# Eight experts as nested conditional blocks of 2x2 products, seven for eight

## The chip, the cores and the metric

The kernel runs on one core of a Trainium2 chip. A core has engines with instruction streams of their own: TensorE for matrix products (PE in the profile, and PEld for the loading of its weights, the operand that stays in the array), VectorE (DVE), ScalarE (ACT), GpSimd (POOL) and SyncE (SP), which here issues transfers. Work moves between memory (DRAM), an on-chip store of 128 partitions (SBUF), and the banks into which TensorE accumulates (PSUM). The metric is the time of one execution on the device in microseconds, the median of several.

## The reference

A sliding-window attention feeds a mixture of experts with one expert per token. Cut to what matters:

```python
q, k, v: (8, 8, 576, 64)                      # batch, heads, positions, head size
scores = q @ k.T / 8, masked to 0 <= i - j < 64
x = softmax(scores) @ v                       # as (4608, 512): one row per token
logits = x @ w_gate                           # (4608, 8)
expert = argmax(logits); gate = softmax(logits)[expert]
for e in range(8):                            # w1[e]: (512, 1024), w2[e]: (1024, 512)
    y[expert == e] = relu(x[expert == e] @ w1[e]) @ w2[e]
out = gate[:, None] * y                       # all in float32
```

With these inputs the experts get 669, 400, 748, 505, 592, 390, 566 and 738 tokens. In chunks of 128 tokens that is 6, 4, 6, 4, 5, 4, 5 and 6, 40 in all. The kernels learn these counts only while they run.

## The kernel before

The program has four stages. The attention computes x for two batches at a time and writes it to DRAM (x_dram); on the way TensorE also forms the logits. The routing, on DVE with some matmuls, ranks the tokens within their experts. Each expert's share starts at a new tile of 128 tokens, so a token's slot is the start of its expert plus its rank; products of one-hot matrices (lo and hi, L467 to L471) give for each slot the token's number (perm_i) and its gate (gate_s). Slots without a token hold a number behind the last token, which the scatter leaves out.

The third stage goes over tiles of 128 slots. For tile i, `fetch` (L497) lets SP read the tile's expert and a flag, and load that expert's w1 and w2 (2 MB each) into one of three buffers where the flag says that the buffer holds another expert (L501, L502); POOL gathers the 128 rows of x by perm_i (L503). `turn` (L508) transposes the rows on TensorE (four transposes, L511), and DVE copies them to SBUF (L512). `work` (L514) computes the hidden layer with its features on the partitions, in two halves of 512 features (32 matmuls of 128 tokens in all; each float32 matmul is two instructions in the profile), applies the relu on DVE for one half (L530) and on ACT for the other (L528), lets TensorE turn the next tile, computes the output (8 matmuls of 512 columns, L535), lets ACT multiply by the gate (L539) and POOL scatter the rows to the output (L541).

There can be up to 43 tiles. The first 36 are written out without a condition; the rest stand in conditional blocks of two tiles (L556), which compare the number of tiles in use with a constant. With 40 tiles in use, the blocks for 36 and 38 run and the ones for 40 and 42 are jumped over.

The order on SP in this stage is as written (manual_schedule); the other engines' order is chosen by the framework's scheduler from what is written and when buffers come free. Tiles name buffers, and the framework puts in the waits between engines.

The fourth stage is the end: the last scatters land, and all engines meet.

## Time and profile before

| what | value |
| --- | --- |
| median of 3 runs (lowest, highest) | 904.05 us (903.75, 904.51) |
| the profiled execution's own time | 907.11 us |
| its span in the profile | 905.4 us |
| granted clock of TensorE, mean | 0.957 |
| attention | 0 to about 262 us |
| routing | about 262 to 312 us |
| tiles of the experts | 312 to 892 us, 580 us |
| end | 892 to 905.4 us |
| TensorE busy over the span | 843.1 us, 93% |
| hidden layer, L523 | 2560 instructions, 294.4 us |
| output, L535 | 640 instructions, 281.3 us |

How to read the profile: the busy time of an engine is the time in which its instructions ran; in a group of instructions the number behind x is the count, then come busy time, the mean of one in ns, and the idle time just before them with what ended it. Matmuls overlap in the pipeline of TensorE, so the mean of one (276 ns for L523) is longer than the distance from one to the next (112 ns in the timeline). The granted clock is 1.00 at full speed; 0.50 is half of it. The span begins with the first instruction and ends with the last; the time of the execution is a little longer.

### The profile page before, as it was taken

The numbers are of one execution on the slowest core, as the hardware profiler recorded it, in microseconds if no ns is written. First come the engines' busy times: TensorE is split into PE (matmuls) and PEld (weight loads), VectorE is DVE, ScalarE is ACT, GpSimd is POOL, SyncE is SP. The second block draws the span as 40 slices with busy tenths as digits, with TensorE's granted clock in tenths as the row PEclk, the third lists the DMA queues.
The fourth block names the chain that finished last, engine by engine and source line by source line (L and its number), as shares of the span: only waits on it lengthen the run. The fifth ranks groups of instructions, "written<-read, shape, count | busy, mean of one in ns | idle before, by whom it ended". The sixth has DMA issues, their size and how long they took to land. (4 is left out here: it accounts for less than half of the span.)

```text
span 905.4 us, 16347 instructions
## 1 busy us (share of the span) xinstructions
PE 843.1 (93%) x6668; PEld 617.7 (68%) x6668; DVE 231.6 (26%) x500; ACT 181.7 (20%) x486; POOL 124.6 (14%) x177
## 2 busy tenths in 40 slices
PE   7997999998953699999999999999999999999993
PEld 5775776776733577686767777686777768677772
DVE  4664665664655000000101000010101001010100
ACT  4553554553510000001000000010000001000000
POOL 3111111011000201111111111111111111101010
PEclk9998999998985599999999999999999999999998
DMA  6668677886020661793951494891794871880110
GB/s 139 150 163 200 142 190 193 212 221 160 3 105 0 235 230 36 280 320 144 315 212 47 148 347 165 308 315 39 240 321 156 314 256 36 316 294 23 36 47 11
DMA packets 164863, 159.99 MB, mean 177 GB/s; under 512 B 118320, under 2 KB 118320, under 8 KB 164786
## 3 DMA queue, kind: packets, MB, share of 16 engines
q1 hardware_dynamic: 153362, 129.01, 45.8%
q0 software_dynamic: 6560, 20.45, 6.2%
q10 hardware_dynamic: 4864, 9.44, 3.1%
q8 instruction: 55, 0.90, 0.4%
q14 instruction: 22, 0.18, 0.1%
HBM read 219.69 MB, written 19.92 MB: 265 GB/s over the span
## 5 line engine op out<-in xcount | busy, mean ns | idle before, releaser
L523 PEld LDWEIGHTS hp<-xgT,w 128*128 128x128 f32 x2560 | 294.1, 193 | 18.8 <-issue 18.7
L523 PE MATMUL hp<-xgT,w 128*128 128x128 f32 x2560 | 294.4, 276 | 0.0
L535 PE MATMUL yp<-w,hT 128*128 128x512 f32 x640 | 281.3, 592 | 0.0
L535 PEld LDWEIGHTS yp<-w,hT 128*128 128x128 f32 x640 | 118.5, 190 | 133.9 <-issue 133.9
L530 DVE TENSOR_SCALAR hT<-hp 128x512 f32<-128x512 f32 x40 | 27.7, 692 | 390.9 <-PE hp L523 390.9
L237 ACT ACTIVATE pr<-sc,mx 128x128 f32<-128x128 f32 x288 | 79.4, 375 | 71.9 <-DVE mx L234 53.3
L528 ACT ACTIVATE hT<-hp 128x512 f32<-128x512 f32 x40 | 23.9, 597 | 310.2 <-PE hp L523 310.2
L541 POOL DMA_INDIRECT out_dram<-y,perm_i x40 | 40.6, 1016 | 316.7 <-ACT y L539 303.2
L539 ACT ACTIVATE y<-yp,gate_s 128x512 f32<-128x512 f32 x40 | 27.5, 687 | 266.1 <-PE yp L535 266.1
L503 POOL DMA_INDIRECT xg<-x_dram,perm_i x42 | 41.0, 975 | 235.6 <-PE tp L511 179.2
L512 DVE COPY xgT<-tp 128x512 f32<-128x512 f32 x41 | 28.3, 691 | 137.2 <-PE tp L511 137.2
L234 DVE TENSOR_REDUCE mx<-sc 128x3 f32<-128x384 f32 x96 | 49.1, 553 | 42.5 <-PE sc L227 41.1
L246 PE MATMUL tr<-ident,pr 128*128 128x128 f32 x288 | 49.5, 287 | 0.1
L246 PEld LDWEIGHTS tr<-ident,pr 128*128 128x128 f32 x288 | 34.7, 146 | 20.1 <-ACT qT L190 7.7
L227 PE MATMUL sc<-kT,qT 64*64 64x128 f32 x1152 | 47.7, 289 | 0.1
L227 PEld LDWEIGHTS sc<-kT,qT 64*64 64x64 f32 x1152 | 34.3, 139 | 13.0 <-issue 8.3
L261 PE MATMUL px<-va,pT 128*64 128x65 f32 x640 | 43.1, 231 | 0.0
L168 POOL COPY vb<-va 64x520 f32<-64x520 f32 x32 | 19.7, 617 | 158.5 <-DMA va<-in_v_dram 144.4
L261 PE MATMUL px<-vb,pT 128*64 128x65 f32 x512 | 41.4, 229 | 0.0
L307 PE MATMUL lg<-xT,wg 128*32 128x384 f32 x96 | 39.9, 498 | 0.7 <-DVE xT L287 0.7
L261 PEld LDWEIGHTS px<-vb,pT 128*64 128x64 f32 x512 | 33.4, 141 | 8.8 <-DVE xT L287 4.0
L261 PEld LDWEIGHTS px<-va,pT 128*64 128x64 f32 x640 | 36.3, 138 | 2.9 <-issue 2.8
(93 smaller groups left out, 476.6 us busy)
## 6 DMA issues: line engine op xcount, KB each, us to landing
w<-in_moe_w_dram SPq DMA_DIRECT2D x86, 2048.0 KB
qs<-in_q_dram SPq DMA_DIRECT2D x64, 128.0 KB
ks<-in_k_dram SPq DMA_DIRECT2D x64, 128.0 KB
va<-in_v_dram SPq DMA_DIRECT2D x64, 128.0 KB
x_dram<-xs ACTq DMA_DIRECT2D x8, 1024.0 KB
qs<-in_q_dram SPq DMA_DIRECT2D x32, 32.0 KB
ks<-in_k_dram SPq DMA_DIRECT2D x32, 32.0 KB
vb<-in_v_dram SPq DMA_DIRECT2D x32, 32.0 KB
```

Of the source, the lines that this page charges most:

```text
L227: nc.tensor.matmul(out_, lhsT=qT[rows, t, a * WINDOW : (a + 1) * WINDOW], rhs=rhs, start=False, stop=True, skip_group_check=True,)
L234: nc.vector.tensor_reduce(out=mx[:], in_=scs[h][:], axis=AX.X, op=ALU.max, negate=True)
L237: nc.scalar.activation(out=pr[:, m, :], in_=scs[h][:, m, :], func=AF.Exp, bias=mx[:, m : m + 1])
L246: nc.tensor.transpose(out=tr[:, m, :], in_=prs[h][:, m, :], identity=ident[:])
L261: nc.tensor.matmul(px[a * D : (a + 1) * D, h, m, :], lhsT=pTs[h][:, m, a * D : (a + 1) * D], rhs=vt[:, h, :], start=True, stop=True, skip_ ...
L307: nc.tensor.matmul(lgs[bg][c * WC : (c + 1) * WC, :], lhsT=wg[:, g, :], rhs=xTs[u][:, c, :], start=(g == 0), stop=(g == NG - 1), skip_grou ...
L503: nc.gpsimd.indirect_dma_start(out=xgs[i % NX][:], out_offset=None, in_=x_dram[:, :], in_offset=bass.IndirectOffsetOnAxis(ap=perm_i[:, i : ...
L512: nc.vector.tensor_copy(out=xgTs[i % 2][:], in_=tp[:])
L523: nc.tensor.matmul(hp[:, f, :], lhsT=w1[:, 0, g, c0 : c0 + P], rhs=xgT[:, g, :], start=(g == 0), stop=(g == NG - 1),)
L530: nc.vector.tensor_scalar_max(hT[:, 0:HF, :], hp[:], 0.0)
L535: nc.tensor.matmul(yp[:], lhsT=hT[:, f, :], rhs=w2[:, 0, f, :], start=(f == 0), stop=(f == FT - 1),)
L541: nc.gpsimd.indirect_dma_start(out=out[:, :], out_offset=bass.IndirectOffsetOnAxis(ap=perm_i[:, i : i + 1], axis=0), in_=y[:], in_offset=N ...
```

## The change

The program is written anew from the routing on, and the weights' handling in part of the attention.

*Blocks.* A tile is now a pair of chunks of 128 tokens, each expert's share starts at a new pair, and the tiles of one expert are written out as nested conditional blocks: `level(t)` asks whether the expert has more than 2t chunks ("some") and then whether it has more than 2t + 1 ("both"). With both, the full body runs and the next level follows inside; with one chunk, a plain body without the scheme below; with none, what is left over of the next expert's weight sums. Four levels are written out for each of the eight experts, and a loop stands behind them that these counts never reach. An expert thus always uses the same buffers, and its weights are loaded once (`load_w`, with two buffers instead of three). Registers now hold the number of chunks and the first tile of the expert, and POOL's index and gate columns are picked by the register.

*Seven products for eight.* In a full body both layers are taken as products of 2x2 blocks, for which a scheme with seven block products and 15 block sums or differences is used. For the hidden layer the blocks of w1 are 256 x 512 and those of x 256 x 128 (two chunks of tokens), so a product is 8 matmuls of 128 columns. For the output the blocks of the hidden layer are 128 tokens x 512 and those of w2 512 x 256, so a product is 4 matmuls of 256 columns. Sums of products are formed partly by accumulating into the same PSUM bank (`product(..., False)`), partly on DVE as the bank is read. The scheme computes the result in another order of additions than before, in float32.

*Sums.* POOL forms the four sums of x after the turn (`sums_x`, 128x256 each), and the eight sums of an expert's weights (128x1024 each) during the previous expert: those of w1 after its first body, those of w2 after the second. For the first expert they are formed inside the attention. DVE forms the four sums of the hidden layer (128x512 each).

*Order.* All engines now work in the order written. Within a body, POOL first scatters the previous tile's result, then copies the gates; later come the sums of x, the gather of the next tile but one, and the weight sums. The scatter of a tile thus stands at the start of the next body, and the last one behind the last expert.

In the changed program the block sums on POOL are issued at L119, those of the hidden layer at L638, L639, L646 and L649, the products of the output layer and what reads them at L640 to L656: the second product into y at L650 behind the reading of y at L648, the last product into x at L655 behind the reading of x at L654.

In the diff most removed lines, which are shown above, and a few added declarations are left out:

```diff
@@ -61,11 +61,14 @@
-    TB = P
+    TB = 2 * P
+    C = TB // P
     NTILE = (NT + TB - 1) // TB + E - 1
-    NS = NTILE
-    NW = 3
-    NCUT = (NT + TB - 1) // TB
+    NX = NTILE + 4
+    NS = NX * C
+    KT = 4
+    NW = 2
+    NCUT = NT // P
...
+    gate_t = consts.tile([P, NX, C + 1], F32, name="gate_t")
+    chunks_i = consts.tile([P, E], I32, name="chunks_i")
+    tiles_i = consts.tile([P, E], I32, name="tiles_i")
+    starts_i = consts.tile([P, E + 1], I32, name="starts_i")
...
+    V, G = nc.vector, nc.gpsimd
+    HG, HF, HD, HM = NG // 2, FT // 2, FF // 2, DM // 2
+    sums_of = lambda pool, i: (
+        pool.tile([P, 4, HG, HD], F32, name=f"s1_{i}"), pool.tile([P, 4, HF, HM], F32, name=f"s2_{i}")
+    )
+    sums = [sums_of(consts, 0)]
+    def left_sums(eng, s, a11, a12, a21, a22):
+        for n, (a, b, op) in enumerate((
+            (a21, a22, ALU.add), (s[:, 0], a11, ALU.subtract), (a11, a21, ALU.subtract),
+            (a12, s[:, 1], ALU.subtract),
+        )):
+            yield partial(eng.tensor_tensor, out=s[:, n], in0=a, in1=b, op=op)
+    def right_sums(eng, t, b11, b12, b21, b22):
+        for n, (a, b) in enumerate(((b12, b11), (b22, t[:, 0]), (b22, b12), (t[:, 1], b21))):
+            yield partial(eng.tensor_tensor, out=t[:, n], in0=a, in1=b, op=ALU.subtract)
+    def form(ops):
+        for op in ops:
+            op()
+    def w1q(e):
+        w = ws[e % NW][0][:, 0]
+        return [w[:, a * HG : (a + 1) * HG, f * HD : (f + 1) * HD] for f in range(2) for a in range(2)]
+    def w2q(e):
+        w = ws[e % NW][1][:, 0]
+        return [w[:, f * HF : (f + 1) * HF, a * HM : (a + 1) * HM] for f in range(2) for a in range(2)]
+    def sums_w1(e):
+        form(left_sums(G, sums[e % NW][0], *w1q(e)))
+    def sums_w2(e):
+        form(right_sums(G, sums[e % NW][1], *w2q(e)))
+    def load_w(e):
+        nc.sync.dma_start(out=ws[e % NW][0][:], in_=w1v[:, e : e + 1, :, :])
+        nc.sync.dma_start(out=ws[e % NW][1][:], in_=w2v[:, e : e + 1, :, :])
...
@@ -332,8 +378,10 @@
         prs, pTs = {}, {}
         for s in range(-2, N + 4):
             if s == N - 2 * NST:
-                nc.sync.dma_start(out=ws[0][0][:], in_=w1v[:, 0:1, :, :])
-                nc.sync.dma_start(out=ws[0][1][:], in_=w2v[:, 0:1, :, :])
+                load_w(0)
+            if s == N - NST:
+                sums_w1(0)
+                sums_w2(0)
...
+    wp = ctx.enter_context(tc.tile_pool(name="wp", bufs=1))
+    ws.append(weights(wp, 1))
+    sums.append(sums_of(wp, 1))
+    load_w(1)
...
         V.tensor_reduce(out=nt[:], in_=over[:], axis=AX.X, op=ALU.add)
+        V.tensor_copy(out=chunks_i[:], in_=nt[:])
+        V.tensor_reduce(
+            out=nt[:], in_=over[:].rearrange("p e (i c) -> p e i c", c=C)[:, :, :, 0], axis=AX.X, op=ALU.add
+        )
+        V.tensor_copy(out=tiles_i[:], in_=nt[:])
         cum = rt.tile([P, E], F32, name="cum")
         V.tensor_tensor_scan(out=cum[:], data0=ones[:, 0:E], data1=nt[:], initial=0.0, op0=ALU.mult, op1=ALU.add)
         start = rt.tile([P, E], F32, name="start")
         V.tensor_tensor(out=start[:], in0=cum[:], in1=nt[:], op=ALU.subtract)
         V.tensor_scalar_mul(start[:], start[:], float(TB))
...
+        V.memset(starts_i[:, 0:1], 0)
+        V.tensor_copy(out=starts_i[:, 1:], in_=cum[:])
...
         V.tensor_scalar_add(perm_i[:], slots[:, 0, :], float(NT))
-        V.tensor_copy(out=gate_s[:], in_=slots[:, 1, :])
+        by_tile = slots[:, 1, :].rearrange("p (i c) -> p i c", c=C)
+        V.tensor_copy(out=gate_t[:, :, 0:C], in_=by_tile)
+        V.tensor_scalar_mul(gate_t[:, :, C], by_tile[:, :, C - 1], -1.0)
...
-        tc.manual_schedule(engines={mybir.EngineType.SP}),
+        tc.tile_pool(name="mp", bufs=1) as mp,
...
+        xg = [mp.tile([P, DM], F32, name=f"xg{c}") for c in range(C)]
+        xq = mp.tile([P, 2, 2, HG, P], F32, name="xq")
+        xs = mp.tile([P, 4, HG, P], F32, name="xs")
+        hq = mp.tile([P, 2, 2, HF, P], F32, name="hq")
+        hs = mp.tile([P, 4, HF, P], F32, name="hs")
+        p1, u2, u3 = (mp.tile([P, HF, P], F32, name=f"part{i}") for i in range(3))
+        y1a, y1b, v2, v3 = (mp.tile([P, HM], F32, name=f"party{i}") for i in range(4))
+        ys = [mp.tile([P, DM], F32, name=f"y{c}") for c in range(C)]
+        gates = mp.tile([P, 3], F32, name="gates")
+        at_g = mp.tile([P, C], I32, name="at_g")
+        at_s = mp.tile([P, C], I32, name="at_s")
+        tps = [ps_xt.tile([P, NG, P], F32, name=f"tp{i}") for i in range(2)]
+        hps = [ps_h.tile([P, HF, P], F32, name=f"hp{i}") for i in range(3)]
+        yps = [ps_y.tile([P, DM], F32, name=f"yp{i}") for i in range(3)]
...
+        def gather(col):
+            G.tensor_copy(out=at_g[:], in_=perm_i[:, col])
+            for c in range(C):
+                G.indirect_dma_start(
+                    out=xg[c][:], out_offset=None, in_=x_dram[:, :],
+                    in_offset=bass.IndirectOffsetOnAxis(ap=at_g[:, c : c + 1], axis=0),
+                )
+        def scatter(col):
+            G.tensor_copy(out=at_s[:], in_=perm_i[:, col])
+            for c in range(C):
+                G.indirect_dma_start(
+                    out=out[:, :], out_offset=bass.IndirectOffsetOnAxis(ap=at_s[:, c : c + 1], axis=0),
+                    in_=ys[c][:], in_offset=None, bounds_check=NT - 1, oob_is_err=False,
+                )
+        def turn():
+            for c in range(C):
+                for g in range(NG):
+                    nc.tensor.transpose(out=tps[c][:, g, :], in_=xg[c][:, g * P : (g + 1) * P], identity=ident[:])
+                nc.scalar.copy(out=xq[:, :, c], in_=tps[c][:].rearrange("p (a g) s -> p a g s", a=2))
+        def sums_x():
+            form(right_sums(G, xs, xq[:, 0, 0], xq[:, 0, 1], xq[:, 1, 0], xq[:, 1, 1]))
+        relu = partial(nc.scalar.activation, func=AF.Relu)
+        scaled = partial(nc.scalar.activation, func=AF.Copy)
+        def hidden(e):
+            a11, a12, a21, a22 = w1q(e)
+            s = sums[e % NW][0]
+            def product(acc, a, b, first=True):
+                for f in range(HF):
+                    for g in range(HG):
+                        nc.tensor.matmul(
+                            acc[:, f, :], lhsT=a[:, g, f * P : (f + 1) * P], rhs=b[:, g, :],
+                            start=(first and f == 0 and g == 0), stop=(g == HG - 1), skip_group_check=True,
+                        )
+            x, y, z = hps
+            product(x, a11, xq[:, 0, 0])
+            nc.scalar.copy(out=p1[:], in_=x[:])
+            product(y, s[:, 1], xs[:, 1])
+            V.tensor_tensor(out=u2[:], in0=y[:], in1=p1[:], op=ALU.add)
+            product(x, a12, xq[:, 1, 0], False)
+            relu(out=hq[:, 0, 0], in_=x[:])
+            product(y, s[:, 2], xs[:, 2], False)
+            V.tensor_tensor(out=u3[:], in0=y[:], in1=p1[:], op=ALU.add)
+            product(z, s[:, 0], xs[:, 0])
+            V.tensor_tensor(out=hq[:, 1, 1], in0=z[:], in1=u3[:], op=ALU.add)
+            relu(out=hq[:, 1, 1], in_=hq[:, 1, 1])
+            product(x, a22, xs[:, 3])
+            V.tensor_tensor(out=hq[:, 1, 0], in0=u3[:], in1=x[:], op=ALU.subtract)
+            relu(out=hq[:, 1, 0], in_=hq[:, 1, 0])
+            product(z, s[:, 3], xq[:, 1, 1], False)
+            V.tensor_tensor(out=hq[:, 0, 1], in0=z[:], in1=u2[:], op=ALU.add)
+            relu(out=hq[:, 0, 1], in_=hq[:, 0, 1])
+        def output(e):
+            b11, b12, b21, b22 = w2q(e)
+            t = sums[e % NW][1]
+            a11, a12, a21, a22 = hq[:, 0, 0], hq[:, 1, 0], hq[:, 0, 1], hq[:, 1, 1]
+            more = left_sums(V, hs, a11, a12, a21, a22)
+            def product(acc, a, b, first=True):
+                for f in range(HF):
+                    nc.tensor.matmul(
+                        acc, lhsT=a[:, f, :], rhs=b[:, f, :],
+                        start=(first and f == 0), stop=(f == HF - 1), skip_group_check=True,
+                    )
+            lo, hi = slice(0, HM), slice(HM, DM)
+            onto = lambda out, acc, c, more: V.scalar_tensor_tensor(
+                out=out, in0=acc, scalar=gates[:, c : c + 1], in1=more, op0=ALU.mult, op1=ALU.add
             )
...
+            x, w, y = (t[:, lo] for t in yps)
+            next(more)()
+            next(more)()
+            product(x, a11, b11)
+            scaled(out=y1a[:], in_=x, scale=gates[:, 0:1])
+            scaled(out=y1b[:], in_=x, scale=gates[:, 1:2])
+            product(w, a22, t[:, 3])
+            product(x, a12, b21, False)
+            scaled(out=ys[0][:, lo], in_=x, scale=gates[:, 0:1])
+            next(more)()
+            product(y, hs[:, 1], t[:, 1])
+            onto(v2[:], y, 0, y1a[:])
+            next(more)()
+            product(y, hs[:, 2], t[:, 2], False)
+            onto(v3[:], y, 1, y1b[:])
+            product(x, hs[:, 0], t[:, 0])
+            onto(ys[1][:, lo], w, 2, v3[:])
+            onto(ys[1][:, hi], x, 1, v3[:])
+            product(x, hs[:, 3], b22, False)
+            onto(ys[0][:, hi], x, 0, v2[:])
+        def plain_hidden(e):
+            w1 = ws[e % NW][0]
...
-                            hp[:, f, :], lhsT=w1[:, 0, g, c0 : c0 + P], rhs=xgT[:, g, :],
+                            hps[m][:, f, :], lhsT=w1[:, 0, g, c0 : c0 + P], rhs=xq[:, g // HG, 0, g % HG, :],
...
+        def plain_output(e):
+            w2 = ws[e % NW][1]
...
+            scaled(out=ys[0][:], in_=yps[0][:], scale=gates[:, 0:1])
+        def body(e, before, now, after, full, aside=()):
+            scatter(before)
+            G.tensor_copy(out=gates[:], in_=gate_t[:, now])
+            (hidden if full else plain_hidden)(e)
+            turn()
+            sums_x()
+            gather(after)
+            (output if full else plain_output)(e)
+            for op in aside:
+                op()
+        gather(slice(C, 2 * C))
+        turn()
+        sums_x()
+        gather(slice(2 * C, 3 * C))
+        for e in range(E):
+            chunks = nc.values_load(chunks_i[0:1, e : e + 1], min_val=0, max_val=NT // P)
+            at = G.value_load(starts_i[0:1, e : e + 1], min_val=0, max_val=NTILE)
+            if 1 < e + 1 < E:
+                load_w(e + 1)
+            asides = [partial(sums_w1, e + 1), partial(sums_w2, e + 1)] if e + 1 < E else []
+            def place(i):
...
+                return bass.ds(i * C, C), bass.ds(i + 1, 1), bass.ds((i + 3) * C, C)
+            def level(t, left):
+                if t == KT:
+                    tiles = nc.values_load(tiles_i[0:1, e : e + 1], min_val=0, max_val=NTILE)
+                    with tc.For_i(KT, tiles) as i:
+                        body(e, *place(at + i), True)
+                    return
+                with tc.If(chunks > 2 * t) as some:
+                    with tc.If(chunks > 2 * t + 1) as both:
+                        body(e, *place(at + t), True, left[:1])
+                        level(t + 1, left[1:])
+                    with both.Else():
+                        body(e, *place(at + t), False, left)
+                with some.Else():
+                    for op in left:
+                        op()
+            level(0, asides)
+        end = G.value_load(starts_i[0:1, E : E + 1], min_val=0, max_val=NTILE)
+        scatter(bass.ds(end * C, C))
```

## The prediction

> **What bounds the kernel now.** I read the page first, then a table of busy time by stretch, then the timeline of TensorE for one tile. The page gives the share of each engine and the span in 40 slices (22.6 us each):
>
> ```profile
> PE 843.1 (93%) x6668; PEld 617.7 (68%) x6668; DVE 231.6 (26%) x500; ACT 181.7 (20%) x486; POOL 124.6 (14%) x177
> ...
> PE   7997999998953699999999999999999999999993
> ...
> POOL 3111111011000201111111111111111111101010
> PEclk9998999998985599999999999999999999999998
> ...
> L523 PE MATMUL hp<-xgT,w 128*128 128x128 f32 x2560 | 294.4, 276 | 0.0
> L535 PE MATMUL yp<-w,hT 128*128 128x512 f32 x640 | 281.3, 592 | 0.0
> ```
>
> TensorE is full from slice 15 on at the full clock, and the two matmul groups of the experts make up 575.7 us; nothing idles before them. The table by stretch says the same (columns: PE, weight loads, DVE, ACT, POOL with counts; granted clock; DMA share; GB/s). First all of the expert stage, then two tiles of it:
>
> ```profile
> 312.00:892.00 580.00, 579.76 (x3357) 426.35 (x3356) 55.32 (x80) 50.88 (x80) 75.97 (x77) 1.00 0.56 196
> 848.25:877.15 28.90, 28.90 (x170) 21.25 (x169) 2.77 (x4) 2.57 (x4) 3.98 (x4) 1.00 0.11 37
> ```
>
> So the stage is 40 tiles of 14.45 us on TensorE alone; all else is cover. A tile on the timeline of TensorE (start, length, line, count):
>
> ```profile
> 848.25 7.31 PE L523 MATMUL hp<-xgT,w 128*128 128x128 f32 x64
> 855.39 0.60 PE L511 MATMUL tp<-ident,xg 128*128 128x128 f32 x4
> 855.83 7.03 PE L535 MATMUL yp<-w,hT 128*128 128x512 f32 x16
> ```
>
> Hidden 7.14 us for 64 instructions (0.1116 each), turn 0.44 for 4, output 6.87 for 16 (0.4294 each).
>
> The profiled execution took 907.11 us, 3.06 over the median of 904.05; its span is 905.4, the other 1.7 lie around it. I sum differences against the span and put them on the median.
>
> **The change part by part.**
>
> **Products.** The counts of tokens give 40 chunks of 128 as before: 19 pairs and 2 single chunks (experts 4 and 6 have odd counts). A pair cost 28.90 us. Now hidden is 7 products of 16 instructions: 112 x 0.1116 = 12.50. The turn is 8 instructions, 0.88. Output is 7 x 8 instructions of half the columns: 56 x 0.4294/2 = 12.02. Sum 25.40, so -3.50 a pair, **-66.5** for 19. Weight loads stay behind the matmuls (0.19 us against 0.215).
>
> **Evacuations in a body.** A product that accumulates into a bank which another engine must read first has to wait. In hidden another product (1.79 us) always lies between, which covers a read of 128x512 (0.69 on DVE, L530). In output two have none: the second product into y (lines of the changed program: L650, right behind the read into v2 of L648) and the last one into x (L655, behind the read of L654). Each wait is 0.2 from PE's end to DVE's start, a read of 128x256 (0.42, halfway down from 0.556 for 128x384 and 0.69 for 128x512), and 0.11 back: 0.73. Two in 19 bodies: **+27.7**. Ends: 0.3 (handover alone) and 1.0 (the full-width read), +11 and +38. The hidden sums on DVE (four of 128x512) start as the relus end and are needed three or four products later; by the order of the program hs[1] is there 3.1 us after hidden ends and needed 6.05 after it, so they cost nothing; if ACT were 3 us late, output would wait for it. Single chunks do 7.14 + 6.87 with a turn of 0.88 instead of 0.44: +0.44 x 2, **+0.9**.
>
> **Weights.** SP loads them once per expert instead of three times (86 issues of 2 MB in before, of which 48 carried data, eight experts into three buffers; now 16). TensorE waited for no load in the expert stage, so nothing is gained. An expert lasts over 50 us, and its 4 MB take 14 us at the 300 GB/s of the busy slices; nothing lost.
>
> **Conditional blocks.** In before, blocks were taken whole and fell through. Now an expert that ends on a full pair skips the rest of its nest: experts 0, 1, 2, 3, 5 and 7. The built program has every engine wait for its own earlier work before the skipped counts are added, so TensorE drains, then makes two taken jumps over about 1,000-1,500 and 400-600 instructions. Five such ends lie inside the stage. The rows nearest: comparisons that fell through at the Ifs of before cost 0.04-0.44 us; a register load 0.49; taken jumps to nearby code 0.46 on DVE, 0.51 on ACT, 0.13 on POOL; behind TensorE's jump at 885.45-885.80 a fetch of instructions starts 0.7 later and takes 0.88 (q8 has 55 packets of 16 KB, 1.05 us each as a mean). If the target is never at hand, a jump is 0.35 + 0.7 + 0.95 = 2.0 us. Two, with load, comparisons and the waits for DVE's and ACT's counts, less the 1.3 us that the sequencer runs ahead, leave TensorE idle for about 4.0. Then the clock. TensorE's longest pause in the attention, and three stretches: behind that pause, a stretch half idle, and behind a pause of 2.69 us:
>
> ```profile
> 84.70 0.48 PE L206 MATMUL sc<-mask,ident_b 128*128 128x384 bf16 x1 [4.80 <-ACT pr L237]
> ```
>
> ```profile
> 84.20:90.90 6.70, 5.91 (x44) 4.13 (x45) 1.51 (x4) 2.42 (x8) 0.51 (x1) 0.50 0.69 164
> 145.60:148.90 3.30, 1.67 (x12) 0.84 (x12) 0.50 (x2) 2.38 (x8) 1.39 (x3) 1.00 1.08 268
> 210.50:217.10 6.60, 6.36 (x60) 4.96 (x60) 2.37 (x5) 1.89 (x6) 1.01 (x2) 0.50 0.70 159
> ```
>
> The clock is 0.50 for 6.8 us after the first and the third, and for 3.41 after the second (its row is the stretch before). Half clock for 6.8 us loses 3.4, for 3.4 us 1.7. Between these I take 2.7. So an end costs 4.0 + 2.7 = 6.7, and five **+33.5**. The low end: jumps as to nearby code and no half clock, 0.9 each, +4.5. The high end: four fetches in a row and 3.4 for the clock, 9 each, +45. I take the upper part because 0.90 MB for 16,347 instructions is 55 bytes each, so the code skipped is one to five fetches of 16 KB, which speaks for a fetch at every target.
>
> The Trainium skill's "TensorE: Matmul & The Clock Gate" (practical rule) warns only of gaps over about 3 us. In this trace 2.69 was enough; by the page's rule the plain ends below would be free of the clock's part, some 2.6 less, and the sum 908. Its "Runtime: NRT & Kernel Launch" (Instruction fetch mechanics) says that a taken branch out of the two pages held must fetch the page before it goes on; it speaks against this change; no row of before shows such a far jump on TensorE, and by its near jumps alone the sum would be 882.
>
> **Plain ends.** Experts 4 and 6 leave from the plain block, one jump each. In these blocks POOL has extra semaphore increments before its DMAs (1.8 us each in the tail of before), so the copy of the gates for the next body may come 2 to 2.5 us late for y1a. Jump, gates and half of the clock's loss (1.3): 4.5 each, **+9** (0 to +20).
>
> **POOL.** Per body: copy of indices, two scatters (1.0 us each by L541), the second behind the landing of the first (2.8 to 8.3 us in before), the gates, four sums of x (L119), two gathers, and in the first two bodies of an expert four weight sums of 128x1024. The row nearest is the copy of 64x520 in 0.617, of 64x390 in 0.507: 0.85 ns per element. With one stream that makes 1.05 a sum, with two reads 2.0, with three passes 2.8; I take 2.0, since the operation reads two tiles. The lag this puts on POOL in a body is 4 x 2.0 - 5.5 = 2.5 us; the gates still come before y1a asks for them 15.45 us into the body. Cost 0 here. If a sum takes more than 2.8 us inside an expert (2.3 to 3.3 at its end, where the next expert waits for POOL's count), every us beyond costs TensorE 4 us in each of some 14 bodies. The first expert's sums run in the attention beside the vb copies, which have 30 us to spare: 0, within 3.
>
> The Trainium skill's "GPSIMD Engine Reference" (Engine selection) speaks against the change too: a two-input operation takes about twice as long on GpSimd as on VectorE, 4497 ns for 2048 elements; as an estimate from that page 2.25 us for 1024, near my value, and the sum would stay the same.
>
> **Routing, start, tail.** Three operations on hi of 128x1548 at 1.77 us become 128x2088, +1.7; the expert id and load flags of the tiles go, about -1.4; chunk and tile counts come, +0.9, the first tile's copies +0.3: **+1.5**. Behind the last matmul the span now runs 13.4 us (scatter, two 1.8 us increments, drain). The second scatter will wait for the first's landing, the increments go: **+1** (-1 to +3).
>
> **Sum.** -66.5 + 27.7 + 0.9 + 33.5 + 9 + 1.5 + 1 = +7.1: span 912.5, median 911.
>
> **The rivals.**
>
> *Cheap jumps (faster).* The targets are fetched ahead or the clock stays up, so an end costs 0.9 to 3 instead of 6.7 and the plain ends about 1 each. The sum is -66.5 + 27.7 + 0.9 + 4.5 to 15 + 2 + 2.5 = -29 to -18: 875 to 886. For it: the Ifs in before cost TensorE nothing that the rows show. Against it: they were not far jumps. With the plain ends as forecast, it decides at (66.5 - 27.7 - 0.9 - 9 - 2.5)/5 = 5.3 us an end: below that the change is faster.
>
> *POOL becomes the bound (slower still).* At 4 us a sum (1.2 beyond the limit) 1.2 x 4 x 14 = 67 and more: about 980; at 3.1 us 928. For it: no two-input operation on POOL in the trace, and DVE reads SBUF far more than before. Against it: DVE's 556 ns (L270) are the same beside POOL's copies as without them.
>
> *The evacuations are dearer than 0.73*, because the pauses pull the clock down in each body. The stretch 145.6 to 148.9 shows that short pauses can, but there TensorE was idle for half of 3.3 us; here 1.5 in 25 us. At a half clock of 3.4 us in each of 19 bodies, 1.7 x 19 = 32 more: 943.
>
> **How the numbers follow.** Forecast as worked out 0.45, with its own range 895 to 925; cheap jumps 0.27; POOL 0.23; evacuations 0.05. The upper part of POOL's case, over 955, is left out, and the little below 875: 875 to 955. A measurement here can tell 0.2% (1.8 us) from no change. Faster takes the 0.27 of cheap jumps and about a quarter of the forecast's own range: 0.38; same 0.05; slower 0.57.
>
> **What would show it.** In the profile after: full bodies of 25.4 + 1.5 = 26.9 us on TensorE with two gaps of about 0.7 at the products of L650 and L655; idle gaps of about 4 us at five expert ends with PEclk down behind them; POOL sums of about 2 us each. Wrong it would be if the gaps at the ends are under 2 us or the clock stays at 1.00 behind them, if POOL's sums are over 2.8 us and TensorE waits for the gates or for POOL at the starts of experts, or if a body is longer than 27.5 us for another reason.

## The result and the profile after

The changed kernel takes 935.12 us (median of 4 runs, 932.53 to 937.34), the kernel before in the same job 904.28: a ratio of 1.0336 (95% interval 1.0305 to 1.0368), 31 us slower. The forecast was 911, 7 us slower. The profiled execution took 937.34 us with a span of 935.6, 30.2 more than the span of before; the sums below are made between these two spans.

The page of the changed kernel, cut to the lines that answer to those of before:

```profile
span 935.6 us, 17237 instructions
...
PE 798.5 (85%) x6832; PEld 674.6 (72%) x6832; DVE 383.6 (41%) x687; ACT 237.6 (25%) x606; POOL 371.1 (40%) x402
...
PE   6999998999914799879699969969989969989992
...
PEclk9999998999956899989989989979999979999997
...
L627 PE MATMUL yp<-s,hs 128*128 128x256 f32 x456 | 106.6, 383 | 12.3 <-DVE party L634 12.3
L595 PE MATMUL hp<-xq,w 128*128 128x128 f32 x608 | 84.9, 299 | 36.5 <-PEq L698 36.3
...
L627 PE MATMUL yp<-w,hs 128*128 128x256 f32 x152 | 37.9, 392 | 13.5 <-DVE y L634 13.5
```

TensorE is busy for 45 us less than before, and yet the span is longer: the row of TensorE, full before from slice 15 on, now has holes (6, 7, 8), and behind some of them the granted clock dips. Three groups have idle time in front of them where before there was none. The view of who waited for whom, TensorE alone (total us, times, longest), gives their sum:

```profile
PE hp L595 <- PEq L698: 36.3, 5, 8.0
...
PE yp L627 <- DVE y L634: 13.5, 19, 0.8
PE yp L627 <- DVE party L634: 12.3, 19, 0.7
...
PE hp L664 <- issue: 4.8, 3, 1.6
```

Five waits, one for each expert that is left by skip, ended by TensorE's own sequencer (PEq) and not by another engine; two waits in each of the 19 full bodies, for VectorE's reading; three short ones in the plain blocks. On the timeline of TensorE, a body and an expert's end (start, length, what, and in brackets the idle time before it):

```profile
341.15 1.95 PE L595 MATMUL hp<-xq,w 128*128 128x128 f32 x16
...
359.71 1.89 PE L627 MATMUL yp<-s,hs 128*128 128x256 f32 x8
362.24 3.72 PE L627 MATMUL yp<-s,hs 128*128 128x256 f32 x16 [0.65 <-DVE party L634]
366.72 1.99 PE L627 MATMUL yp<-w,hs 128*128 128x256 f32 x8 [0.76 <-DVE y L634]
368.55 1.95 PE L595 MATMUL hp<-xq,w 128*128 128x128 f32 x16
...
393.95 1.99 PE L627 MATMUL yp<-w,hs 128*128 128x256 f32 x8 [0.58 <-DVE y L634]
403.91 3.75 PE L595 MATMUL hp<-xq,w 128*128 128x128 f32 x16 [7.97 <-PEq L698]
```

A body takes 368.55 - 341.15 = 27.40 us. At the end of the first expert TensorE stands for 7.97 us, and the first product after it takes 3.75 instead of 1.95: half clock, as the table by stretch shows (the pause, then what follows it; the clock is the number behind POOL's):

```profile
395.94:403.91 7.97, 0.00 (x2) 0.03 (x1) 0.48 (x1) 0.00 (x0) 1.51 (x2) 0.83 0.57 211
403.91:407.80 3.89, 3.89 (x18) 3.89 (x19) 0.00 (x0) 0.05 (x1) 0.70 (x2) 0.50 1.01 378
```

What the sequencer did in the pause is in the view of line L716, the comparisons of "some", in this window and in that of the second end (count; shortest, median and longest in ns; first and last start):

```profile
L716 PEldq COMPARE_BRANCH  x2: 3872/4334/4796, 394.0 to 398.3; - x2
...
L716 PEldq COMPARE_BRANCH  x2: 3273/3298/3324, 459.0 to 462.6; - x2
```

Two taken branches one after the other, 3.3 to 4.8 us each. The first is issued 2.0 us before TensorE's last matmul ends. In the packets of the queue that fetches instructions (times in us, all packets of 16 KB between 393 and 404) each branch has its own:

```
branch 393.97 to 397.84   fetch 394.98, 1.41 us
branch 398.27 to 403.07   fetch 398.58, 1.44 us; fetch 400.67, 1.07 us
```

So a branch with one fetch takes 3.3 to 3.9 us, one with two about 4.8. At the second end (pause 5.87) both branches had one fetch each; at the other four the second had two (4.5 to 5.0 us). That these packets are TensorE's is read from the times and the sizes: in the kernel before, this queue moved 0.90 MB for TensorE's 13,609 instructions, and another, in packets of 8 KB, 0.18 MB for the other engines' 2,738, 66 bytes each in both cases.

The span by terms, from the starts of the bodies in the trace:

| term | forecast | measured |
| --- | --- | --- |
| 19 pairs, matmuls alone (28.90 to 25.40 each) | -66.5 | -65.2 (to 25.47, from the second experiment) |
| two readings per body | +27.7 | +36.0 (with known counts, experiment 1 against 6) |
| plain bodies, second turn | +0.9 | +0.9 |
| five ends by skip | +33.5 | +49.8 |
| two plain ends | +9 | +5.7 |
| routing and start | +1.5 | +0.1 (-0.3 before the first body, +0.4 of half clock in it) |
| tail | +1 | +2.6 |
| sum | +7.1 | +29.9 (spans: +30.2) |

### The profile page after: what moved, and what is told of

Its sections match the earlier page's. It is cut to its first block, busy times and chain, and to the rows that moved or that the text cites. A ratio compares the mean times of both kernels' runs of the same rounds, so it can differ in the third digit from the quotient of the medians.

```text
span 935.6 us, 17237 instructions
## 1 busy us (share of the span) xinstructions
PE 798.5 (85%) x6832; PEld 674.6 (72%) x6832; DVE 383.6 (41%) x687; ACT 237.6 (25%) x606; POOL 371.1 (40%) x402
## 5 line engine op out<-in xcount | busy, mean ns | idle before, releaser
L627 PE MATMUL yp<-s,hs 128*128 128x256 f32 x456 | 106.6, 383 | 12.3 <-DVE party L634 12.3
L595 PE MATMUL hp<-xq,w 128*128 128x128 f32 x608 | 84.9, 299 | 36.5 <-PEq L698 36.3
L595 PE MATMUL hp<-xs,s 128*128 128x128 f32 x912 | 112.5, 282 | 0.0
L595 PEld LDWEIGHTS hp<-xq,w 128*128 128x128 f32 x608 | 81.6, 214 | 40.4 <-issue 39.6
L595 PEld LDWEIGHTS hp<-xs,s 128*128 128x128 f32 x912 | 109.9, 199 | 0.0
L627 PEld LDWEIGHTS yp<-s,hs 128*128 128x128 f32 x456 | 85.1, 190 | 30.7 <-DVE party L634 19.9
L119 POOL TENSOR_TENSOR xs<-xq 128x256 f32<-128x256 f32 x44 | 36.9, 838 | 159.0 <-ACT xq L580 159.0
L119 POOL TENSOR_TENSOR s<-w 128x1024 f32<-128x1024 f32 x32 | 75.3, 2355 | 12.6 <-DMA w<-in_moe_w_dram 12.4
L627 PE MATMUL yp<-w,hq 128*128 128x256 f32 x304 | 71.9, 379 | 0.0
L604 DVE TENSOR_TENSOR part<-hp,part 128x512 f32<-128x512 f32 x19 | 13.1, 692 | 140.9 <-PE hp L595 129.3
L627 PEld LDWEIGHTS yp<-w,hq 128*128 128x128 f32 x304 | 56.3, 190 | 6.9
L292 PE MATMUL tr<-ident,pr 128*128 128x128 f32 x288 | 49.8, 288 | 0.1
L649 DVE TENSOR_TENSOR hs<-hq,hs 128x512 f32<-128x512 f32 x19 | 48.9, 2575 | 0.0
```

Source lines behind the costliest of these rows:

```text
L119: op()
L292: nc.tensor.transpose(out=tr[:, m, :], in_=prs[h][:, m, :], identity=ident[:])
L595: nc.tensor.matmul(acc[:, f, :], lhsT=a[:, g, f * P : (f + 1) * P], rhs=b[:, g, :], start=(first and f == 0 and g == 0), stop=(g == HG - 1 ...
L604: V.tensor_tensor(out=u2[:], in0=y[:], in1=p1[:], op=ALU.add)
L627: nc.tensor.matmul(acc, lhsT=a[:, f, :], rhs=b[:, f, :], start=(first and f == 0), stop=(f == HF - 1), skip_group_check=True,)
L649: next(more)()
```

## The experiments

Two theories stood first: J, that TensorE's jumps and the half clock behind them make the ends, and W, that the two readings cost what the table says; against them P, that GpSimd holds up the starts of experts, and D, that VectorE is late in any case.

**1. Known counts.** Everything stays but the conditions:

```diff
-            chunks = nc.values_load(chunks_i[0:1, e : e + 1], min_val=0, max_val=NT // P)
-            at = G.value_load(starts_i[0:1, e : e + 1], min_val=0, max_val=NTILE)
...
+        COUNTS = (6, 4, 6, 4, 5, 4, 5, 6)
...
+            for t in range((COUNTS[e] + 1) // 2):
+                full = COUNTS[e] > 2 * t + 1
+                body(e, *place(at + t), full, left[:1] if full else left)
```

> The changed kernel with the eight experts' chunk counts written in as constants: the same bodies in the same order on every engine, no conditional block and no register; it is right for these inputs alone. Theory J (TensorE's far jumps and the half clock behind them make up the ends): the five ends by skip, 49.8 us in the trace of the changed kernel, and the two plain blocks' 6.6 go, so about 935 - 56 = 879 us, and the clock stays at 1.00 from the second body on. Rival P (GpSimd holds up the starts of experts: its scatters, gates and weight sums are the same here): the pauses at expert starts stay and the time is over 915.

Measured: 878.0 us, ratio 0.971 (0.969 to 0.974) to the kernel before. TensorE's waits that are left in the expert stage are the readings:

```profile
PE yp L627 <- DVE y L634: 13.2, 19, 0.8
PE yp L627 <- DVE party L634: 12.6, 19, 1.0
```

GpSimd does the same work in the same order, and no expert's start waits for it: P falls. The span is 59.0 us shorter than with conditions (876.6): the ends' 49.8, the plain blocks' 5.7, 2.7 in the tail (13.6 after the last matmul instead of 16.3), and less than 1 elsewhere.

**2. Products in turns.** The output's last four products alternate between two banks:

```diff
             next(more)()
+            next(more)()
             product(y, hs[:, 1], t[:, 1])
             onto(v2[:], y, 0, y1a[:])
-            next(more)()
+            product(x, hs[:, 0], t[:, 0])
+            onto(v4[:], x, 1, y1b[:])
             product(y, hs[:, 2], t[:, 2], False)
             onto(v3[:], y, 1, y1b[:])
-            product(x, hs[:, 0], t[:, 0])
+            onto(ys[1][:, hi], y, 1, v4[:])
             onto(ys[1][:, lo], w, 2, v3[:])
-            onto(ys[1][:, hi], x, 1, v3[:])
             product(x, hs[:, 3], b22, False)
             onto(ys[0][:, hi], x, 0, v2[:])
```

> The changed kernel with the last four products of the output layer taken in turns on two banks (y, x, y, x), so that each bank is read while the other product runs, and with all four sums of the hidden layer formed ahead of them. Theory W (two uncovered readings of PSUM cost 0.92 and 1.03 us in each of 19 bodies): a body goes from 27.39 to about 25.45 us and the time to 935 - 37 = 898. Rival D (VectorE is late anyway, since its sum at L649 takes 2.6 us on average beside GpSimd's sums instead of 0.69): the waits only move, the body stays over 26.5 us and the time over 918.

Measured: 892.8 us, ratio 0.988 (0.986 to 0.991): 1.2% faster than the kernel before. On its timeline the output runs through:

```profile
336.84 1.95 PE L595 MATMUL hp<-xq,w 128*128 128x128 f32 x16
...
353.67 1.89 PE L627 MATMUL yp<-w,hq 128*128 128x256 f32 x8
355.40 5.34 PE L627 MATMUL yp<-s,hs 128*128 128x256 f32 x24
360.58 1.89 PE L627 MATMUL yp<-w,hs 128*128 128x256 f32 x8
362.31 0.94 PE L595 MATMUL hp<-xq,w 128*128 128x128 f32 x7
```

A body is now 362.31 - 336.84 = 25.47 us, which is the forecast's 25.40 for the matmuls alone; W holds with 1.93 us a body (1.76 in the five without weight sums). Most of the rest of the gain, some 6 us, comes from the ends, with 32.1 us of waits instead of 36.3 and 10.6 us lost to the half clock instead of 12.8: the branch is now issued earlier before TensorE's end (2.8 us at the first expert).

**3. No weight sums in the expert stage.**

```diff
-            asides = [partial(sums_w1, e + 1), partial(sums_w2, e + 1)] if e + 1 < E else []
+            asides = []
...
-            s = sums[e % NW][0]
+            s = sums[0][0]
...
-            t = sums[e % NW][1]
+            t = sums[0][1]
```

> The changed kernel without the weight sums in the expert stage: every expert uses the first expert's sums, so the output is wrong for the others; all else is the same. Theory J: TensorE waits for none of these sums; only the slowed sum at L649 goes back to 0.69 us, which takes 0.18 us from the second wait in 14 bodies: 935 - 2.5 = 932.5. Rival P (GpSimd's load makes the ends long): the five ends fall by 3 us or more each and the time is under 921.

Measured: 931.1 us, ratio 1.030 (1.027 to 1.034), 4 us less than with them. The waits at the ends are 35.8 us instead of 36.3. VectorE's last sum of the hidden layer, in the changed kernel and then in this one:

```profile
L649 DVE TENSOR_TENSOR hs<-hq,hs 128x512 f32<-128x512 f32 x19 | 48.9, 2575 | 0.0
```

```profile
L649 DVE TENSOR_TENSOR hs<-hq,hs 128x512 f32<-128x512 f32 x19 | 12.9, 680 | 0.0
```

P falls for the second time, for this kernel. GpSimd's sums do slow VectorE's, by 1.9 us each, but almost all of that is hidden.

**4. Jumps by distance, in the kernel before.** Behind eight of its tiles stands a block that is never taken:

```diff
+        SKIPS = {3: 4, 7: 32, 11: 96, 15: 288, 19: 4, 23: 32, 27: 96, 31: 288}
...
             work(i, True)
+            if i in SKIPS:
+                with tc.If(used > NTILE - 1):
+                    yp = ps_y.tile([P, DM], F32, name="yp")
+                    for r in range(SKIPS[i]):
+                        nc.tensor.matmul(
```

> The kernel before, with conditional blocks that are never taken behind eight of its tiles: they hold 4, 32, 96, 288, 4, 32, 96, 288 matmuls in this order (four instructions each). It measures the price of a jump on TensorE by its distance. Theory J: the branch over 4 matmuls takes under 0.6 us on TensorE, the ones over 96 and 288 take 3.3 us (one fetch of 16 KB of instructions) or about 4.8 (two), the ones over 32 lie at either price; TensorE's pause is that less what its sequencer runs ahead. Rival (the price is the draining and counting at the end of a block, whatever the distance): all eight take the same within 0.3 us.

The branches of TensorE at L556, all eight and then in order, from the same view in narrower windows:

```profile
L556 PEldq COMPARE_BRANCH  x8: 208/340/5257, 358.2 to 769.2; - x8
```

| matmuls jumped over | 4 | 32 | 96 | 288 |
| --- | --- | --- | --- | --- |
| first time, us | 0.24 | 0.36 | 1.15 | 5.26 |
| second time, us | 0.24 | 0.21 | 0.33 | 3.49 |

The rival, one price for every block, falls. The two longest jumps cost what the ends' branches cost, and only behind them does TensorE stand, for 2.65 and 0.88 us. But 96 matmuls cost 1.15 and 0.33, where theory J had 3.3. They are some 24 KB of code by estimate, as a full body is with 92 matmuls: in experiment 6, without conditions, the 516 us of 19 full and two plain bodies fetched 28 pages of 16 KB, so some 22 KB a full body and half of that a plain one. Here, out of code that runs straight on, that far was still at hand: no packet of 16 KB falls into the two branches. The time was 909.9 us in one run, against 903.8.

**5. Blocks side by side.** If distance were the price, short jumps would be cheap. In the kernel of experiment 2:

```diff
-                with tc.If(chunks > 2 * t) as some:
-                    with tc.If(chunks > 2 * t + 1) as both:
-                        body(e, *place(at + t), True, left[:1])
-                        level(t + 1, left[1:])
...
+            for t in range(KT):
+                aside = asides[t : t + 1]
+                with tc.If(chunks > 2 * t + 1) as both:
+                    body(e, *place(at + t), True, aside)
...
+            with tc.If(chunks > 2 * KT):
...
+            with tc.If(odd > 0):
+                body(e, *place(at + last - 1), False)
```

> The kernel of the second experiment (products in turns) with its blocks side by side instead of nested: one block per full tile (three, then the loop for more), and one plain block behind them, so that a jump passes over 24 KB of TensorE's instructions (a full body) or 12 KB (the plain block) at most; experts still read their counts while they run. Theory J (the price is the distance to the target): in the kernel with blocks over the old tiles, branches over 32 and 96 matmuls took 0.2 to 1.2 us, so an end by skip falls from 9.1 us to about 3, with less of the half clock: 893 - 30 = 863, at most 875. Rival Q (several short jumps in a row reach code as little at hand as one far jump, 3.3 us each): ends stay at 8 us or more and the time over 888.

Measured: 912.7 us, ratio 1.009 (1.006 to 1.013): 20 us slower than nested, with two more register loads for each expert. Theory J in the form of distance falls, and the rival stands. TensorE's branches at the three kinds of blocks (full body, loop, plain block):

```profile
L724 PEldq COMPARE_BRANCH  x42: 70/171/3890, 336.5 to 889.3; - x42
```

```profile
L729 PEldq COMPARE_BRANCH  x8: 2840/3483/3803, 387.6 to 889.7; - x8
```

```profile
L733 PEldq COMPARE_BRANCH  x10: 82/2698/3115, 391.8 to 893.8; - x10
```

Jumps over the loop (some 24 KB) take 2.8 to 3.8 us, three of the eight out of running code (3.5 to 3.8) and five right after another jump. Jumps over the plain block (12 KB), right after another jump, take 2.7 to 3.1 in the six cases where it is skipped. All of these have one fetch each. Over a full body, out of running code, three of five took 3.3 to 3.9 us and two 0.35 and 0.37. So at the same distance a jump may miss or not. What counts is whether its target's page has been fetched; that running on fetches the page ahead, and a jump leaves nothing ahead, would explain the three rows, and is theory F.

**6. Both of 1 and 2.**

> Known counts as constants and the products in turns, both edits at once; right for these inputs alone. If the two costs are independent, the gains add: 878.0 - 1.93 x 19 = 841 us. If the waits in the output layer had hidden something that comes late (the sums of x on GpSimd, the gathers), the body stays over 25.8 us and the time over 848.

Measured: 842.7 us, ratio 0.931 (0.928 to 0.933). The gains add, and the seven products are worth 62 us over the kernel before (904.5 in the same job) where nothing stands in their way; this version has the counts written in.

**7. Full bodies only.** In the kernel of experiment 2 the plain blocks go, so that behind the first jump's target lie only a few short blocks:

```diff
                 with tc.If(chunks > 2 * t) as some:
-                    with tc.If(chunks > 2 * t + 1) as both:
-                        body(e, *place(at + t), True, left[:1])
-                        level(t + 1, left[1:])
-                    with both.Else():
-                        body(e, *place(at + t), False, left)
+                    body(e, *place(at + t), True, left[:1])
+                    level(t + 1, left[1:])
```

> The kernel of the second experiment without its plain blocks: an odd last chunk is computed as a full body with an empty half, and nothing but short blocks lies between the first jump's target and the next expert. Theory F (each taken branch of TensorE to a page of instructions that is not at hand waits for its fetch, 3.3 us for one page and about 4.8 for two, whatever the distance): the first branch of an end stays at 3.3 to 3.9 us and the second falls from 3.1-4.9 to under 0.5, so the pause of an end falls from 6.4 to about 2.5 us and with the half clock from 9 to about 4. Seven ends at 4 and 21 full bodies at 25.47: 893 + 2 x (25.5 + 4 - 14.5 - 4) - 5 x 5 = 890 us. Rival C (the second branch is long because of the counts that all engines add at the end, not for a fetch): it stays over 3 us and the time is over 910.

Measured: 896.7 us (893.5 to 899.9), ratio 0.994 (0.992 to 0.996), 7 us over the forecast of 890; the profiled execution is the fastest of the seven, 893.5. The branches at the first end (the third belongs to the next expert) and the timeline there:

```profile
L717 PEldq COMPARE_BRANCH  x3: 77/193/3552, 384.9 to 389.4; - x3
```

```profile
385.76 1.89 PE L627 MATMUL yp<-w,hs 128*128 128x256 f32 x8
389.68 2.02 PE L595 MATMUL hp<-xq,w 128*128 128x128 f32 x16 [2.04 <-PEq L699]
```

The second branch takes 0.19 us instead of 4.9; the pause is 2.04 instead of 7.01. So it was the fetch and not the counting at the end, and theory F holds. The packets of 16 KB say the same. In the nine runs with such branches, 114 of TensorE's branches in the expert stage last over 1 us; 113 have a packet inside, and 106 of these end 1.3 to 1.5 us after their last packet (the others 1.2 to 2.2). No packet starts inside one of the seven second branches of 0.19 us here.

Of the seven pauses, all 2.0 to 2.2 us long, four left the clock at full speed and three halved it for a while (1.7, 3.0 and 3.1 us lost). The time is no better than in experiment 2: two half-empty bodies cost 11 us each over plain ones, and a wait has come that the forecast did not have:

```profile
PE hp L595 <- PEq L699: 14.5, 7, 2.2
...
PE hp L595 <- POOLq L717: 3.9, 3, 1.5
```

Behind the three experts with two full bodies, the next expert's second product waits for GpSimd, whose weight sums and the count behind them end late there (at 446.4 us behind the second expert; TensorE goes on at 446.46). With known counts (experiment 6) the same sums end 3.9 us after the start of the same product, and TensorE does not wait. That speaks for the count at the end of the block, and not the sums, as what holds TensorE: something of C and P comes true once the jumps are cheap.

**8. No waits in the output layer.** In the kernel of experiment 2, the products that alternated get banks of their own:

```diff
+            x0, y2, x3 = (t[:, 0:2, :].rearrange("p f s -> p (f s)") for t in hps)
...
+            product(x0, hs[:, 0], t[:, 0])
             product(y, hs[:, 1], t[:, 1])
...
+            product(y2, hs[:, 2], t[:, 2])
...
+            product(x3, hs[:, 3], b22)
```

> The kernel of the second experiment with the output layer's seven products in seven banks of their own (three of them those of the hidden layer, free by then; VectorE adds with two more operations), so that no product of the output layer waits for a reading. Theory A (TensorE's sequencer reaches the branch at an expert's end as soon as the last wait before it is over, up to a number of queued instructions): the branch is issued 3.4 us (16 matmuls) or more ahead of TensorE's end instead of 2.6, the pause falls by 0.8 us or more in five ends, and the time is 888 us or less, down to 878 if the queue holds more than 16. Rival: the queue's depth already sets the 2.6 us; then nothing changes, 891 to 895.

Measured: 888.5 us, ratio 0.986 (0.982 to 0.990), at the edge of what theory A had. At the first end the branch is issued at 383.53, 4.03 us ahead of TensorE's end (2.8 in experiment 2), so the queue's depth was not the limit there. But the branch itself then took 4.63 us instead of 3.62, because its packet starts 2.27 us after it instead of 1.01; why is open. The pause fell only from 7.01 to 6.71; over the five ends the waits are 28.7 us instead of 32.1, 0.7 an end where theory A had 0.8 or more.

**9. Plain blocks first.** In the kernel of experiment 8 the order of each level's blocks is turned round:

```diff
-                    with tc.If(chunks > 2 * t + 1) as both:
-                        body(e, *place(at + t), True, left[:1])
-                        level(t + 1, left[1:])
-                    with both.Else():
-                        body(e, *place(at + t), False, left)
+                    with tc.If(chunks < 2 * t + 2) as single:
+                        body(e, *place(at + t), False, left)
+                    with single.Else():
+                        body(e, *place(at + t), True, left[:1])
+                        level(t + 1, left[1:])
```

> The kernel of the experiment before (no waits in the output layer) with the order of the blocks turned round: each level's plain block stands before its full body, so that an even expert's last jump passes only short blocks, and each full body is reached by a jump over a plain block (12 KB). Theory F: the second branch of an end falls under 0.5 us as without plain blocks, and the five ends get 5 to 7 us shorter each, -30; the 19 entries to full bodies cost what a 12 KB jump out of running code costs: nothing beyond the draining (0.5 us, +10) where the page is at hand, as after the kernel before's tiles, and 3.3 us less 3.9 of running ahead where it is not: about 870 us. Rival: entered by a jump, a body has no further page at hand, each of the 19 jumps misses and its wait is not covered: 2 us each, about 900.

Measured: 879.6 us, ratio 0.973 (0.968 to 0.978), the fastest version that reads its counts while it runs. Inside the first expert the three branches over plain blocks took this:

```profile
L720 PEldq COMPARE_BRANCH  x3: 320/330/345, 312.6 to 362.0; - x3
```

Bodies that follow one another still take 25.47 us, so a 12 KB jump out of running code is free here, as in experiment 4. The second branch of an end is down to 0.19 us. It missed the forecast's 870 since the jump into the next expert's first body, the second over a block within 6 us, waits for a page whose fetch started only 0.4 to 0.9 us before it: 1.5 to 2.4 us at the five ends, and the pauses are 2.8 to 4.1 us.

**10. Full bodies only and no waits.**

> Full bodies only and no waits in the output layer, both at once. Theory F with A: seven ends with one missed branch each, issued 3.9 us ahead of TensorE's end, pause 2.05 less 0.5 to 1.3 us: 888 to 893. Rival: the pause of 2.05 us is not the branch but the counts that follow it: 895 to 898, as without the second edit.

Measured: 890.0 us, ratio 0.987 (0.983 to 0.992). The pauses at the seven ends are 1.2 to 1.6 us instead of 2.0 to 2.2, so issuing the one branch earlier does shorten them, as F and A together have it. GpSimd takes back part of it: the three waits for its count are 6.8 us instead of 3.9.

## Why the prediction was right and wrong

The direction was right, and so were the mechanisms of every large term; two sizes were off, and together they are the miss (16 and 8 us too little; the other terms nearly cancel).

*Products:* right. 25.40 us for a pair's matmuls was forecast, 25.47 measured once the waits are gone.

*Ends by skip:* the step that failed. "If the target is never at hand, a jump is 0.35 + 0.7 + 0.95 = 2.0 us" took the fetch's start and length from the nearest rows and let execution go on when the packet ended. In the trace a branch with one fetch lasts 3.3 to 3.9 us: at the first end 1.0 passes before the packet starts, the packet takes 1.4, and 1.45 more pass before the branch ends; and four of the five second branches needed two fetches (4.5 to 5.0 us). The pause was to be 4.0 us and was 7.3 on average (36.3 / 5). The clock's part was right: 2.7 forecast, 2.6 on average (2.1 to 3.0). In all 9.96 us an end instead of 6.7, beyond the 9 that the forecast had as its high end. That the jumps would be missed was right. The 55 bytes an instruction behind it divide these packets among all engines; they fit TensorE alone, at 66, which changes little in the count of pages. The reason given, the distance of several times 16 KB, was only half of it, too: experiment 5 showed that 12 KB miss as well right after another jump, and experiment 9 that the same 12 KB do not out of running code.

*Readings:* the mechanism right, the size not. 0.73 us each was forecast; they cost 1.93 together. The wait at L650 shows as 0.65 of idle time and sets the next start back by 0.8, and both waits were followed by one slower step of the next product (0.32 us instead of 0.22). The last one was later still in the bodies with weight sums (0.76 instead of 0.58), since VectorE's sum at L649 was slowed and pushed back what follows it in VectorE's order; the forecast looked at whether a sum would be late for TensorE, not at what else waits behind it.

*Plain ends:* 5.7 instead of 9. There are two waits on entry (1.5 and 1.6 us), where a jump over the full bodies is missed, and one of 1.6 twelve matmuls later, right behind another fetch; the branch out of the plain block takes 6.0 and 3.3 us and is hidden but for 0.2, because it is issued 6.7 us ahead of the end of the output's 16 matmuls of 512 columns. The late gates that were forecast did not show.

*GpSimd:* right. A weight sum takes 2.36 to 2.50 us in the mean (2.0 forecast, limit 2.8); leaving them out gains 4 us of 935. *Routing and start* +0.1 for +1.5 and *tail* +2.6 for +1 are small; the tail's excess goes with the conditions.

*The rivals:* cheap jumps would have needed ends under 5.3 us; they came to that only in experiments 7 and 10, with 4.2 and 3.1 us on average, where the second jump's target was at hand.

## What to carry to other kernels

A skipped block costs TensorE not its length but the pages of instructions that the jump finds missing: some 3 us for each fetch here, in a row when jumps follow one another, and half clock behind a long enough pause. So count the taken jumps on the path rather than the branches in the code, let a second jump land close to the first one's target, and end what comes before with work that waits for nothing. Then look at what the pause had hidden: here it was GpSimd's count. Before trading matmuls for additions, write down for each accumulation who must read the bank first and what TensorE does meanwhile: two such readings took back more than half of the gain from the products, and a different order of the same products removed both.

## What the runs showed of the hardware

A VectorE sum with both operands in SBUF (128x512) takes 0.69 us alone and up to 3.26 beside GpSimd's sums, while VectorE's sums with one operand in PSUM stay at 0.69 throughout (L604 to L616). The one at L646, also with both operands in SBUF, takes 1.22 with the weight sums and without them. The forecast had taken from before that VectorE is not slowed beside GpSimd; that row (L270) reads PSUM. The Trainium skill's "SBUF — State Buffer" (SBUF: two separate sides) states that a VectorE operation with two SBUF inputs and a GpSimd operation that reads SBUF take turns on a port that they share; the third experiment agrees with 2.575 against 0.680 us.

Pauses of TensorE of 2.0 to 2.2 us halved its clock in three cases of seven in experiment 7 (behind two of these three a second wait of about 1 us followed within 3 us, behind the third, of 2.00 us, none), pauses of 5.1 us and more always (ten cases in the changed kernel and experiment 2).
